# Fused attention and gated feed-forward on one core: another written-out order of 5,000 planned steps, other engines for some of them, and another replay behind the fill matmuls

## The chip, the core and the metric

The kernel is one program on one core of a Trainium2 chip. The metric is the device time of one execution in microseconds (us); lower is better. Five engines run their own instruction streams and wait for each other through semaphores: TensorE (PE in the rows; its weight loads are PEld), VectorE (DVE), ScalarE (ACT), GpSimd (POOL) and SyncE (SP), which here issues nearly all transfers.

## The reference

```
scores = q @ k.T / sqrt(64)                       # 8 batches x 8 heads, 576 x 576, head size 64
scores = where(scores >= max(scores) - tau, scores, -1e9)
attn   = exp(scores - max(scores));  attn /= sum(attn) + 1e-9
x = (attn @ v)  -> 4608 tokens x 512
h = x @ w_in                                      # 512 x 2048
g = h if h >= 1, 0 if h <= -1, else (h + 1)**2 / 4
out = g @ w_out                                   # 2048 x 512
```

q, k, v and the output are float32; w_in and w_out come as 64-bit floats.

## The kernel before, in words

Every operand of a matmul is split into a high and a low half-precision part, and each product is the sum of three matmuls (high x high, high x low, low x high). Only the four head pairs of batch 0 take their scores from plain float32 ("exact") products. Scales (powers of two, from sums of squares or from Gram matrices) are worked out for each operand before it is split.

**Attention.** The 8 heads of a batch are 4 pairs p; a pair fills 128 partitions. Scores come in *tiles* of 128 rows x 576, 288 in all (j = 0 to 287), two to a *visit* (144 visits). A tile passes smax (DVE: scale and minimum, L1127), sthr (DVE or ACT: threshold), sexp (ACT, L1137), smask (DVE: mask and sum, L1151), a normalisation, shi (ACT, high part, L1177), slo (low part, L1180) and a transposing DMA into eT (L1213). The letter of the tile in the table TILE says where normalisation and low part run: P (the default) normalises on POOL (snorm, L1169) after a reciprocal on DVE, and subtracts on POOL; N normalises on ACT after two small operations on DVE and subtracts on POOL; V takes the high part with the scale on ACT and the low part in one DVE instruction (lo_v, L1210). Then PE multiplies with V (L1299, "av"), and ACT and DVE write the result as two parts into an x buffer.

**V.** Four raw blocks of a batch (128 x 576, float32) are loaded, a scale is worked out (letter of the batch in SSQV: A = four squares on ACT with their sums, L685; G = Gram matrices on PE, L553, and a maximum on DVE, L691), and each block is split. Batch 0 is turned by PE instead (turn_v, L760, into the two score banks s0 and s1, evicted by ACT L765 and DVE L769).

**q and k** of batches 1 to 7 are scaled likewise (SSQ, one letter for each pair) and split: P on POOL (scale L645, low part L658), D with the low part on DVE (L656).

**Weights.** w_in and w_out come in 16 units of 512 KB each. ACT, POOL and DVE rebuild float32 from the bits (L853, L860, L862, L868, L870), PE takes Gram matrices (L881), one scale is worked out for each quarter of w_in and one for w_out (L786 to L794), and CONV says how each unit is split: A (scale and high part on ACT, L922 and L928; low part on POOL, L933), G (the same with scale and high part on POOL, L924 and L930), P and Q (high part on POOL, the difference by PE, L942 and L943, evicted by ACT, L949, or DVE), D (high part on POOL, L936, low part on DVE, L939) and M (scaled by PE, L952; ACT L955 and DVE L958 read it out).

**Feed-forward.** Tokens go in groups of 256. FFN1 (PE, ph<-x,WI) feeds relu and square (ACT L1376, L1379), the gate (DVE L1383) and its two parts (ACT L1388, DVE L1393); FFN2 (PE, acc<-WO) accumulates, ACT evicts (L1438) and SP stores. Before relu of batch b the factors fcs of the batch are needed (f_scale, five small operations, L1026 to L1030; letter in FSCALE: G on POOL, V on DVE).

**What sets the order.** Each step is an op of a planner (class Plan) with an engine, a cost, what it follows and which buffers it takes. The table ORDER lists all ops. The planner replays them in that order with its costs, and the program is written out sorted by the start times that this replay gives, so every engine executes its ops in that order. Where the replay shows TensorE idle for more than 0.4 us in the first 120 us, *fill matmuls* of ones x ones (keep_warm, L1454) are put in, 75% of the gap's length, into a bank of PSUM that is free there.

Of the kernel before, what the change touches and what calls it, by code (L numbers as in the profile page):

```python
# [24 lines left out]
XJ, XS = 1.2, 1.0  # L25

CONV = {"i": "AGAGGAGGPAGAADDP", "o": "PDDAADMGAAQGAGAD"}

# [1482 lines left out]
```

## Time and profile before

| | |
|---|---|
| three runs | 1097.62, 1098.51, 1099.12 us (median 1098.51) |
| profiled execution, first to last instruction | 1097.3 us (it has no other time of its own) |
| mean granted TensorE clock | 0.993 |
| PE busy | 1073.0 us, 98% |
| DVE, ACT, POOL busy | 906.1, 871.2, 759.4 us |
| fill matmuls | 314, of which 265 into the ph banks take 20.2 us |
| DMA | 155.88 MB moved, mean 142 GB/s |

The page says how long each engine worked, but the stages differ: in the first 40 us the transfers move nearly 400 GB/s, later less than half of that; and the three engines DVE, ACT and POOL, which have slack over the whole span, have little in the first 143 us. So the windows are read first, then the order of events in the first 143 us.

### The profile page before, as it was taken

The page shows a single profiled execution, that of the slowest core. Times are in us where ns is not written, and L with a number is a line of the kernel's source. Part 1 is how long each engine was busy: PE and PEld are TensorE (multiplying, and loading weights), DVE is VectorE, ACT ScalarE, POOL GpSimd, SP SyncE. Part 2 cuts the span into 40 slices and gives each one's busy share as a digit, 9 for nine tenths or more (in the row PEclk, how much of TensorE's full clock was granted, in tenths as well). Part 3 has the DMA queues.
Part 4 walks back from the last instruction along what each step waited for, and adds up shares of the span by engine and source line. Part 5 has one row for each costly group of instructions (what it writes and reads, how often), then busy time and mean ns, then how long its engine had stood idle before and what let it go on. Part 6 is the DMA issues. An engine that isn't in the chain of part 4 may idle for free.

```text
span 1097.3 us, 36713 instructions
## 1 busy us (share of the span) xinstructions
PE 1073.0 (98%) x14591; PEld 790.6 (72%) x14591; DVE 906.1 (83%) x2651; ACT 871.2 (79%) x1682; POOL 759.4 (69%) x880
## 2 busy tenths in 40 slices
PE   8799999999999999999999999999999999999998
PEld 7477668777777777776777677777786677767774
DVE  5899999999888888988898998888887899877223
ACT  5999989897888897887798888778788986776333
POOL 5999998786678785897668776576567885565000
PEclk9799999999999999999999999999999999999999
DMA  9997899775977887787778788569856676557000
GB/s 352 332 256 143 139 188 141 152 140 115 191 140 141 152 152 127 135 150 137 139 142 146 150 128 147 113 127 164 151 102 120 131 128 127 105 95 132 18 15 20
DMA packets 420668, 155.88 MB, mean 142 GB/s; under 512 B 399504, under 2 KB 399504, under 8 KB 420496
## 3 DMA queue, kind: packets, MB, share of 16 engines
q1 hardware_dynamic: 420416, 153.41, 71.7%
q8 instruction: 114, 1.87, 0.7%
q14 instruction: 58, 0.48, 0.2%
q10 hardware_dynamic: 80, 0.13, 0.0%
HBM read 45.09 MB, written 9.44 MB: 50 GB/s over the span
## 4 chain that ended last, share of the span: by engine, by line
PE 80%; DVE 10%; DMA 5%; POOL 2%; issue 2%; ACT 1%; SPq 0%; DVEq 0%; POOLq 0%; ACTq 0%
PE acc L466 30%; PE ph L466 30%; PE s L1073 9%; PE ph L1299 9%; DMA eT<-hl 2%; DVE s L1127 2%; DVE e L1151 2%; POOL hl L1180 1%; PE ph L1454 1%; DMA qq<-in_q_dram 1%; DMA kk<-in_k_dram 1%; DMA raw<-in_v_dram 1%; DVE ph L1383 1%; POOL e L1169 0%; DVE WO L939 0%
## 5 line engine op out<-in xcount | busy, mean ns | idle before, releaser
L466 PEld LDWEIGHTS <-WI 128*64 128x64 f16 (+1 forms) x7446 | 407.3, 108 | 55.1 <-issue 18.3
L1180 POOL TENSOR_TENSOR hl<-e,hl 128x576 f16<-128x576 f32 x267 | 347.3, 1309 | 107.7 <-ACT hl L1177 101.8
L466 PE MATMUL ph<-x,WI 128*64 128x256 f16 (+1 forms) x6912 | 400.6, 264 | 2.3 <-DVE x L1311 0.9
L1169 POOL TENSOR_SCALAR e<-e,sm 128x576 f32<-128x576 f32 x259 | 203.5, 790 | 106.6 <-DVE sm L1161 75.3
L1151 DVE SCALAR_TENSOR_TENSOR e<-s,sm,e 128x578 f32<-128x578 f32 x286 | 229.9, 812 | 21.6 <-ACT e L1137 17.0
L1137 ACT ACTIVATE e<-s,sm 128x576 f32<-128x576 f32 x288 | 208.5, 739 | 40.4 <-DVE s L1127 36.4
L1127 DVE TENSOR_SCALAR_CACHE_REDUCE s<-s,pc 128x576 f32<-128x576 f32 x252 | 203.5, 820 | 36.6 <-PE s L1073 35.3
L1177 ACT ACTIVATE hl<-e 128x576 f16<-128x576 f32 x267 | 178.2, 680 | 44.1 <-POOL e L1169 41.1
L466 PE MATMUL acc<-WO,ga 128*64 128x512 f16 (+1 forms) x1590 | 203.4, 380 | 0.0
L1073 PE MATMUL s<-kk,qq 64*128 64x288 f16 (+3 forms) x1840 | 152.1, 300 | 9.9 <-DMA qq<-in_q_dram 5.2
L466 PEld LDWEIGHTS <-ga 128*64 128x64 f16 (+1 forms) x1590 | 91.2, 109 | 82.3 <-issue 9.9
L1383 DVE SCALAR_TENSOR_TENSOR ph<-ph,fcs,asq 128x512 f32<-128x512 f32 (+1 forms) x160 | 111.7, 700 | 46.1 <-ACT asq L1379 44.9
L1376 ACT ACTIVATE asq<-ph,fcs 128x512 f32<-128x512 f32 (+1 forms) x160 | 116.1, 736 | 37.7 <-PE ph L466 36.9
L1299 PE MATMUL ph<-eT,vst 128*64 128x320 f16 (+2 forms) x1928 | 122.7, 279 | 2.9 <-DMA eT<-hl 2.0
L1299 PEld LDWEIGHTS <-vst 128*64 128x64 f16 x1928 | 100.2, 110 | 22.9 <-issue 7.9
L1073 PEld LDWEIGHTS <-qq 64*128 64x128 f16 (+1 forms) x1680 | 66.2, 96 | 48.3 <-issue 35.6
L1388 ACT ACTIVATE ga<-ph,fcs 128x256 f16<-128x256 f32 (+1 forms) x160 | 70.2, 450 | 29.2 <-DVE ph L1383 22.4
L1379 ACT ACTIVATE asq<-asq 128x512 f32<-128x512 f32 x144 | 90.3, 629 | 3.2
L1393 DVE SCALAR_TENSOR_TENSOR ga<-ph,fcs,ga 128x256 f16<-128x256 f32 (+1 forms) x160 | 70.5, 449 | 23.7 <-ACT WI L1388 8.3
L466 PE MATMUL acc<-WO,gb 128*64 128x512 f16 (+1 forms) x546 | 71.0, 379 | 0.0
L466 PE MATMUL acc<-WO 128*64 128x512 f16 (+1 forms) x546 | 69.4, 380 | 0.0
L466 PE MATMUL acc<-WO,WI 128*64 128x512 f16 (+1 forms) x534 | 68.2, 380 | 0.0
(189 smaller groups left out, 1162.5 us busy)
## 6 DMA issues: line engine op xcount, KB each, us to landing
raw<-in_v_dram SPq DMA_DIRECT2D x32, 288.0 KB, 3.5
WO<-in_moe_w_in_dram SPq DMA_DIRECT2D x16, 512.0 KB, 8.6
out_dram<-ob SPq DMA_DIRECT2D x32, 256.0 KB, 2.8
raw<-in_q_dram SPq DMA_DIRECT2D x28, 288.0 KB, 3.4
raw<-in_k_dram SPq DMA_DIRECT2D x28, 288.0 KB, 3.5
x<-in_moe_w_out_dram SPq DMA_DIRECT2D x10, 512.0 KB, 7.0
eT<-hl SPq DMA_TRANSPOSE x288, 3.5
WO<-in_moe_w_out_dram SPq DMA_DIRECT2D x4, 512.0 KB, 4.3
```

What stands on the lines that cost most here:

```text
L466: T.matmul(out[x], lhsT[:, x], rhs, **flags)
L1073: T.matmul(ap(sb, s_ps)[r, f, :SH], q, k, start=ql == kl == 0, stop=exact or ql == 1)
L1127: V.tensor_scalar(sv(), sv(), c, None, ALU.mult, ALU.min, accum_out=t[:, 0:1])
L1137: A.activation(ev(), sv(), AF.Exp, bias=ap(m, sm)[:, 0:1], scale=-1.0)
L1151: V.scalar_tensor_tensor(ev(SH + 1), sv(SH + 1), t[:, 2:3], ev(SH + 1), ALU.is_le, ALU.mult, accum_out=t[:, 3:4])
L1169: G.tensor_scalar(ev(), ev(), ap(m, sm)[:, 5:6], ESC, ALU.mult, ALU.mult)
L1177: A.activation(part2(0), ev(), AF.Copy)
L1180: G.tensor_tensor(part2(w), ev(), part2(0), ALU.subtract)
L1299: T.matmul(o[hd * D : (hd + 1) * D, :n], vt[:, k, hd * D : (hd + 1) * D], t[:, kb, (hd ^ p % 2) * n : ((hd ^ p % 2) + 1) * n], start=m == ...
L1376: A.activation(tv()[:, :, c], hv()[:, :, c], AF.Relu, bias=fcs[:, b, 2, q : q + 1], scale=fcs[:, b, 3, q : q + 1])
L1379: A.activation(ap(tb, asq), ap(tb, asq), AF.Square)
L1383: V.scalar_tensor_tensor(hv()[:, :, c], hv()[:, :, c], fcs[:, b, 0, q : q + 1], tv()[:, :, c], ALU.max, ALU.min)
```

## The change

All of ORDER is replaced, and so are the letters of the tables; the planner gets other costs and three more rules.

- **Letters.** CONV: units of kind A go from 12 to 7, G from 9 to 14, P from 3 to 1, Q from 1 to 0, D from 6 to 7, M from 1 to 3 (both weights together). TILE: N from 8 to 64 tiles, V from 19 to 27, P from 259 to 195 (among the 36 tiles of batch 0, which come first: N from 8 to 10, V from 3 to 2). The exact scores of batch 0 (visits 0 to 17) have 5 visits in two halves (S) instead of 9; of the others none instead of 2. QHOW now has a letter each for q and k: 25 of 64 are D, before it was 8 of 32 pairs, in batch 1 four of eight instead of two of eight. V gets its own table VHOW: G as before, A with the high part on ACT, P with scale and low part on POOL. SSQV: batch 0 takes its V scale from ACT instead of PE. SSQ: pairs 8 and 21 take theirs from Gram matrices on PE instead of ACT. FSCALE: batch 0 on DVE. SIGN and THR change too.
- **Replay.** The hop from one engine to the next depends on both; an op marked port (the low parts on DVE that read two SBUF operands: lo_v, the D parts of q, k and weights, V's) and any op of POOL exclude each other in time; after a long gap of TensorE that no free bank allows to be filled, its ops cost 85% more for 5 us.
- **Fill.** The first gap is filled to half of the former share; a bank that nobody takes later counts as free to the end. There are 403 fill matmuls instead of 314.

```
-XJ, XS = 1.2, 1.0
-CONV = {"i": "AGAGGAGGPAGAADDP", "o": "PDDAADMGAAQGAGAD"}
-PAIR = "SJSJSJSSJSSSSJJJJJSJJJJJJJJJJJJSJJJJJJJJJJJJJJJJJJJJJJJJJJJJJJJJJJJJJJJJJJJJJJJJJJJJJJJJJJJJJJJJJJJJJJJJJJJJJJJJJJJJJJJJJJJJJJJJJJJJJJJJJJJJJJJJ"
-QHOW = "DDPDPPDPPPDDPPPPPPPPPPPPPDDPPPPP"
+XJ, XS = 1.2, 1.17
+CONV = {"i": "GAGGGDGGPGGAADDA", "o": "GADMDGMGGAMGDAGD"}
+PAIR = "JJSSJJSJJSSJJJJJJJJJJJJJJJJJJJJJJJJJJJJJJJJJJJJJJJJJJJJJJJJJJJJJJJJJJJJJJJJJJJJJJJJJJJJJJJJJJJJJJJJJJJJJJJJJJJJJJJJJJJJJJJJJJJJJJJJJJJJJJJJJJJJJ"
+VHOW = "GGGGGPGGGPGGGGPGAAPAGGGAGGGG"
+QHOW = "DDDDPPDDPDPPDDDPPDPPPDPPDPDDPPPDPPPPPDPPPDDPPPDPPDPPDDPDPPPPPPPD"
...
 ORDER = [
-    0, 605, 606, 607, 608, 609, 12, 16, 13, 17, 1, 14, 18, 15, 19, 20, 21, 590, 592, 22, 23, 595, 580, 582, 591, 585, 587, 2, 593, 600, 611, 616, 596,
+    15, 19, 12, 16, 13, 17, 14, 574, 18, 0, 1, 20, 21, 847, 22, 584, 589, 585, 586, 576, 575, 577, 591, 23, 24, 26, 25, 579, 581, 38, 39, 41, 40, 42,
...
-SSQ = "AAAAAAAAAAAAAAAAAAAAAAAAAAAAAAAA"
-SSQV = "GAAAAAAA"
+SSQ = "AAAAAAAAGAAAAAAAAAAAAGAAAAAAAAAA"
+SSQV = "AAAAAAAA"
...
-FSCALE = "GGGGGGGG"
+FSCALE = "VGGGGGGG"
...
-    HOP = {"PE": 0.21, "DVE": 0.16, "ACT": 0.17, "POOL": 0.1, "SP": 0.08}
-    FREE, QUEUE, TURN, PAUSE = 0.18, 6.5, 0.097, (3.4, 2.2)
+    HOP = {
+        "PE": {"PE": 0.0, "DVE": 0.21, "ACT": 0.21, "POOL": 0.21, "SP": 0.21},
+        "DVE": {"PE": 0.15, "DVE": 0.14, "ACT": 0.17, "POOL": 0.24, "SP": 0.13},
+        "ACT": {"PE": 0.15, "DVE": 0.14, "ACT": 0.14, "POOL": 0.18, "SP": 0.14},
+        "POOL": {"PE": 0.08, "DVE": 0.08, "ACT": 0.06, "POOL": 0.12, "SP": 0.05},
+        "SP": {"PE": 0.12, "DVE": 0.08, "ACT": 0.05, "POOL": 0.08, "SP": 0.0},
+    }
+    FREE, QUEUE, TURN, PAUSE = 0.18, 6.5, 0.097, (3.4, 0.8)
...
-    def op(self, eng, cost, fn, after=(), take=(), uses=(), work=None, behind=None, mode=0):
+    def op(self, eng, cost, fn, after=(), take=(), uses=(), work=None, behind=None, mode=0, port=False):
 
         o = Op(eng, cost, fn, work, mode)
+        o.port = port
         o.n = len(self.ops)
...
+        busy, alone, slow = (0.0, 0.0), (0.0, 0.0), 0.0
         for o in self.ops:
             o.t = 0.0
         for o in (self.ops[n] for n in ORDER):
                 free[b.pool].remove(x)
                 b.slot, b.end = x[1], 0.0
                 t = max(t, x[0])
+            if o.port and t + o.cost > busy[0]:
+                t = max(t, busy[1])
+            elif o.eng == "POOL" and t + o.cost > alone[0]:
+                t = max(t, alone[1])
             o.t = t
             for b in o.take:
                 b.since = t
-            end = idle[o.eng] = t + o.cost
+            end = t + o.cost
+            if o.eng == "PE" and t < 120:
+                if t - idle["PE"] >= 2.2 and not any(x[0] <= idle["PE"] + 0.4 for p in ("ph", "acc", "s") for x in free[p]):
+                    slow = t + 5.0
+                if t < slow:
+                    end += 0.85 * o.cost
+            idle[o.eng] = end
+            if o.port:
+                alone = t, end
+            elif o.eng == "POOL":
+                busy = t, end
             if o.eng == "PE":
                 turn, mode = self.turned(mode, o.mode)
                 end = idle[o.eng] = end + self.TURN * turn
                     free[b.pool].append((b.end + self.FREE, b.slot))
                     self.held.append((b.pool, b.slot, b.since, b.end + self.FREE))
             for x in o.next:
-                x.t = max(x.t, end + (self.HOP[o.eng] if x.eng != o.eng else 0.0))
+                x.t = max(x.t, end + self.HOP[o.eng][x.eng])
...
-            def hi(rb=rb, tb=tb):
-                G.tensor_scalar(ap(tb, vb)[:, : 2 * S].rearrange("p (a s) -> p a s", a=2),
-                                ap(rb, raw)[:, None, :].to_broadcast([P, 2, S]), s[:, 2:3], 1.0, ALU.mult, ALU.mult)
-
-            def lo(rb=rb, tb=tb):
+            def norm(rb=rb):
+                G.tensor_scalar(ap(rb, raw), ap(rb, raw), s[:, 2:3], 1.0, ALU.mult, ALU.mult)
+
+            def hi(how, rb=rb, tb=tb):
+                t = ap(tb, vb)[:, : 2 * S].rearrange("p (a s) -> p a s", a=2)
+                r = ap(rb, raw)[:, None, :].to_broadcast([P, 2, S])
+                if how == "G":
+                    G.tensor_scalar(t, r, s[:, 2:3], 1.0, ALU.mult, ALU.mult)
+                elif how == "A":
+                    A.activation(t, r, AF.Copy, scale=s[:, 2:3])
+                else:
+                    A.activation(t, r, AF.Copy)
+
+            def lo(how, rb=rb, tb=tb):
                 t = ap(tb, vb)
-                V.scalar_tensor_tensor(t[:, 2 * S : 3 * S], ap(rb, raw), s[:, 2:3], t[:, :S], ALU.mult, ALU.subtract)
+                if how == "P":
+                    G.tensor_tensor(t[:, 2 * S : 3 * S], ap(rb, raw), t[:, :S], ALU.subtract)
+                else:
+                    V.scalar_tensor_tensor(t[:, 2 * S : 3 * S], ap(rb, raw), s[:, 2:3], t[:, :S], ALU.mult, ALU.subtract)
 
             def send(tb=tb, ob=ob):
                 Y.dma_start_transpose(ap(ob, vst), ap(tb, vb))
 
-            o1 = plan.op("POOL", 1.197, hi, [so], take=[tb], uses=[rb])
-            o2 = plan.op("DVE", 1.2 if b == 1 else 1.1, lo, [o1], uses=[rb, tb])
-            o3 = plan.op("SP", 1.65, send, [o2], take=[ob], uses=[tb], work=VSEND)
+            done = []
+            for how in plan.ways(("v", 4 * b + p - 4), VHOW[4 * b + p - 4], "GAP"):
+                o = plan.op("POOL", 0.712, norm, [so], uses=[rb]) if how == "P" else so
+                o = plan.op(*(("POOL", 1.197) if how == "G" else ("ACT", 1.14 if how == "A" else 1.05)), partial(hi, how), [o], take=[tb], uses=[rb])
+                done.append(plan.op(*(("POOL", 1.25) if how == "P" else ("DVE", 0.7)), partial(lo, how), [o], uses=[rb, tb], port=how != "P"))
+            o3 = plan.op("SP", 1.7, send, [plan.join(done)], take=[ob], uses=[tb], work=VSEND)
...
-            gap = WARM[2] * (o.t - free)
+            gap = WARM[2] * (o.t - free) * (0.5 if free < 3 else 1)
             if o.t - free > WARM[0] and o.t < WARM[1]:
                 until = {}
                 for p, x, bank in banks:
-                    until[p, x] = min([t0 for q, y, t0, t1 in plan.held if (q, y) == (p, x) and t1 > free] + [o.t])
+                    until[p, x] = min([t0 for q, y, t0, t1 in plan.held if (q, y) == (p, x) and t1 > free] + [1e9])
```

The first ACTIVATE rows of ACT, as the program lists them. Before (ph, WO and x are stages of weight units, vst and s the turned V of batch 0):

```order
L862 ACT_TABLE_LOAD
L862 ACTIVATE ph0_63<-WO_68 128x512
L503 ACTIVATE junk_128<-ones_129 128x1
L853 ACTIVATE ph2_65<-WO_68 128x512
L853 ACTIVATE WO_68<-WO_68 128x512
L862 ACTIVATE ph0_63<-WO_68 128x512
L853 ACTIVATE ph1_64<-WO_68 128x512
L765 ACTIVATE vst0_85<-s0_61 128x512
L765 ACTIVATE vst0_85<-s0_61 64x128
L853 ACTIVATE ph2_65<-WO_68 128x512
```

And now, at the same place (line numbers are those of the changed kernel, 21 to 37 higher):

```order
L707 ACT_TABLE_LOAD
L707 ACTIVATE junk_128,vssq_143<-raw0_69 128x576
L707 ACTIVATE junk_128,vssq_143<-raw1_70 128x576
L707 ACTIVATE junk_128,vssq_143<-raw2_71 128x576
L707 ACTIVATE junk_128,vssq_143<-raw3_72 128x576
L525 ACTIVATE junk_128<-ones_129 128x1
L890 ACTIVATE WO_68<-WO_68 128x512
L899 ACTIVATE ph1_64<-WO_68 128x512
L890 ACTIVATE ph2_65<-WO_68 128x512
L899 ACTIVATE ph0_63<-WO_68 128x512
L802 ACTIVATE vst0_85<-s0_61 128x512
L802 ACTIVATE vst0_85<-s0_61 64x128
```

The four squares of V now stand ahead of all weight units on ACT; on PE the four Gram matrices of V are gone.

The queue of SP from the first load of q or k to the load of the third pair's q (qq_82; kk and qq are the four exact pairs, raw the blocks of V, WO and x stages of weight units). Before, behind 8 weight units and the 4 blocks of V:

```order
L571 DMA kk_76<-in_k_dram 128x576
L571 DMA qq_80<-in_q_dram 128x576
L839 DMA WO<-in_moe_w_in_dram 128x1024 x3
L571 DMA qq_81<-in_q_dram 128x576
L571 DMA kk_77<-in_k_dram 128x576
L839 DMA WO<-in_moe_w_in_dram 128x1024
L839 DMA x_107<-in_moe_w_out_dram 128x1024
L839 DMA x_105<-in_moe_w_out_dram 128x1024
L839 DMA WO<-in_moe_w_in_dram 128x1024 x3
L571 DMA kk_78<-in_k_dram 128x576
L571 DMA qq_82<-in_q_dram 128x576
```

And now, behind the 4 blocks of V, which come first of all, and 7 weight units:

```order
L593 DMA qq_80<-in_q_dram 128x576
L535 DMA tcs<-in_tau_dram 128x1
L593 DMA qq_81<-in_q_dram 128x576
L593 DMA kk_76<-in_k_dram 128x576
L876 DMA WO<-in_moe_w_in_dram 128x1024 x2
L876 DMA x_105<-in_moe_w_out_dram 128x1024
L876 DMA WO<-in_moe_w_in_dram 128x1024
L593 DMA kk_77<-in_k_dram 128x576
L593 DMA kk_78<-in_k_dram 128x576
L876 DMA WO<-in_moe_w_in_dram 128x1024
L593 DMA qq_82<-in_q_dram 128x576
```

Up to and with qq_82 the queue held 8 + 3 + 1 + 2 + 3 = 17 weight units of 512 KB and 4 + 6 = 10 blocks of 288 KB; now it holds 7 + 2 + 1 + 1 + 1 = 12 units and the same 10 blocks.

## Rows read from the trace of the kernel before

**Rows 1.** Windows of the span: busy us (instructions), granted clock, DMA share, GB/s.

```profile
0.00:20.00 20.00, 17.20 (x209) 15.46 (x210) 7.93 (x22) 9.22 (x18) 8.95 (x47) 1.00 0.92 336
20.00:40.00 20.00, 14.02 (x113) 10.13 (x110) 17.86 (x56) 18.57 (x35) 17.45 (x22) 0.84 1.11 395
40.00:60.00 20.00, 16.66 (x173) 12.26 (x172) 18.16 (x64) 18.76 (x36) 19.31 (x22) 0.81 1.06 292
60.00:100.00 40.00, 37.18 (x551) 29.93 (x549) 36.82 (x111) 38.33 (x82) 38.27 (x53) 1.00 0.89 187
100.00:143.00 43.00, 40.45 (x419) 27.10 (x418) 40.78 (x113) 39.09 (x75) 41.26 (x40) 1.00 0.91 158
143.00:1098.00 955.00, 947.46 (x13141) 695.67 (x13138) 784.60 (x2291) 747.24 (x1442) 634.13 (x700) 1.00 0.69 127
```

**Rows 2.** Who PE waited for from 143 us to the end.

```profile
PE ph L1299 <- DMA eT<-hl: 1.6, 3, 0.8
PE s L1073 <- DVE e L1151: 0.5, 2, 0.3
```

**Rows 3.** Timeline of SP from 1 to 3 us: start, us, what.

```profile
1.20 1.83 SPq L680 DMA_DIRECT2D raw<-in_v_dram  x4
```

**Rows 4.** DMA issues from 1.1 to 3.1 us: KB each, median us to landing.

```profile
raw<-in_v_dram SPq DMA_DIRECT2D x4, 288.0 KB, 5.6
```

**Rows 5.** Timeline of PE, first 60 us.

```profile
10.91 0.65 PE L553 MATMUL ph<-raw 128*128 128x128 bf16 x5
...
35.78 3.27 PE L1073 MATMUL s<-kk,qq 64*128 64x288 f32 x8 [5.21 <-DMA qq<-in_q_dram]
```

**Rows 6.** Timeline of DVE at the scale of V.

```profile
11.60 0.29 DVE L691 TENSOR_REDUCE vssq<-ph 128x1 f32<-128x128 f32 x1 [3.07 <-PE ph L553]
```

**Rows 7.** Timeline of POOL: first split of a weight, first f_scale.

```profile
21.69 0.69 POOL L924 TENSOR_SCALAR WI<-WI,wsc_i 128x512 f32<-128x512 f32 x1 [2.68 <-DVE wsc_i L794]
...
63.60 0.26 POOL L1026 TENSOR_SCALAR scs<-scs,wsc_i 128x1 f32<-128x1 f32 x1
...
64.78 0.22 POOL L1030 TENSOR_TENSOR fcs<-wsc_i,fk 128x16 f32<-128x16 f32 x1
```

**Rows 8.** Groups by line: count, busy us, mean ns of one, idle before.

```profile
L1180 POOL TENSOR_TENSOR hl<-e,hl 128x576 f16<-128x576 f32 x267 | 347.3, 1309 | 107.7 <-ACT hl L1177 101.8 <-issue 4.1 <-POOL e L1169 0.7
...
L1454 PE MATMUL ph<-ones 128*128 128x128 bf16 x265 | 20.2, 237 | 2.9 <-POOL ones L487 2.8
...
L685 ACT ACTIVATE junk<-raw 128x576 f16<-128x576 f32 x28 | 19.2, 685 | 1.4 <-DMA raw<-in_v_dram 1.4
...
L685 ACT ACTIVATION_READ_ACCUMULATOR junk<-raw 128x1 f32 x28 | 5.6, 202 | 0.0
...
L922 ACT ACTIVATE WI<-WI,wsc_i 128x512 f32<-128x512 f32 x6 | 4.3, 712 | 1.0 <-DVE wsc_i L794 1.0
...
L924 POOL TENSOR_SCALAR WI<-WI,wsc_i 128x512 f32<-128x512 f32 x6 | 4.2, 697 | 2.8 <-DVE wsc_i L794 2.7
...
L928 ACT ACTIVATE WI<-WI 128x512 f16<-128x512 f32 x6 | 3.7, 622 | 0.2
...
L939 DVE SCALAR_TENSOR_TENSOR WO<-WO,wsc_o 128x512 f16<-128x512 f32 x4 | 5.9, 1463 | 0.1
...
L939 DVE SCALAR_TENSOR_TENSOR WI<-WI,wsc_i 128x512 f16<-128x512 f32 x2 | 1.6, 804 | 0.0
...
L958 DVE TENSOR_TENSOR WO<-ph,WO 128x512 f16<-128x512 f32 x1 | 0.7, 684 | 0.0
```

**Rows 9.** V's low part on DVE, all instructions: ns min/median/max, first and last start.

```profile
L733 DVE SCALAR_TENSOR_TENSOR vb<-raw,scs,vb x28: 798/854/1940, 111.7 to 939.2; 128x576 f16<-128x576 f32 x28
```

**Rows 10.** Timeline of PE from 60 to 100 us.

```profile
65.38 2.10 PE L1073 MATMUL s<-kk,qq 64*128 64x288 f32 x8
...
80.07 1.54 PE L881 MATMUL acc<-WO 128*128 128x128 bf16 x24
...
82.84 1.24 PE L1073 MATMUL s<-kk,qq 64*128 64x288 f32 x8
```

More of the change, by code (lines that the diff above doesn't have):

```diff
@@ L660, in add_qk @@
             o2, o3 = [], []
-            for how in plan.ways(("qk", at), QHOW[at], "PD"):
-                o1 = plan.op("POOL", 0.724, norm, [sc1], uses=[rb, cb]) if how == "P" else sc1
-                o2.append(plan.op("ACT", 0.582 if how == "P" else 0.67, partial(hi, how), [o1], take=[nb], uses=[rb, cb]))
-                o3.append(plan.op(*(("POOL", 1.245) if how == "P" else ("DVE", 0.8)), partial(lo, how), [o2[-1]], uses=[rb, nb, cb]))
+            for how in plan.ways(("qk", 2 * at + n), QHOW[2 * at + n], "PD"):
+                o1 = plan.op("POOL", 0.712, norm, [sc1], uses=[rb, cb]) if how == "P" else sc1
+                o2.append(plan.op("ACT", 0.573 if how == "P" else 0.666, partial(hi, how), [o1], take=[nb], uses=[rb, cb]))
+                o3.append(plan.op(*(("POOL", 1.25) if how == "P" else ("DVE", 0.7)), partial(lo, how), [o2[-1]], uses=[rb, nb, cb], port=how != "P"))
             o2, o3 = plan.join(o2), plan.join(o3)
@@ L707, in add_v @@
                 for p in range(NPAIR):
-                    o = plan.op("PE", 0.29, partial(gram, p), [loads[p], o], take=[] if p else [sb], uses=[bufs[p], sb])
+                    o = plan.op("PE", 0.487, partial(gram, p), [loads[p], o], take=[] if p else [sb], uses=[bufs[p], sb])
                 o = plan.op("DVE", 0.2, largest, [o], uses=[sb])
@@ L769, in lo @@
                     V.tensor_tensor(t[:r, nk + k0 : nk + k1], view()[:r, k0:k1], t[:r, k0:k1], ALU.subtract)
-                h = plan.op("ACT", (k1 - k0) * P / 1200 + 0.05, hi, [o], take=[] if k0 else [ob], uses=[tb, ob], behind=h)
+                h = plan.op("ACT", (k1 - k0) * P / 1200 + 0.062, hi, [o], take=[] if k0 else [ob], uses=[tb, ob], behind=h)
                 done.append(plan.op("DVE", (k1 - k0) * P / 960 + 0.065, lo, [h], uses=[tb, ob]))
@@ L908, in add_w @@
                 gbuf = plan.buf("acc")
-            stats.append(plan.op("PE", 0.243, gram, [o4], take=[gbuf] if not u else [], uses=[gbuf], behind=stats[-1] if stats else None))
+            stats.append(plan.op("PE", 0.232, gram, [o4], take=[gbuf] if not u else [], uses=[gbuf], behind=stats[-1] if stats else None))
         wscale[w] = []
@@ L974, in add_w @@
                     if how == "D":
-                        done.append(plan.op("DVE", 1.1, rest2, [o]))
+                        done.append(plan.op("DVE", 0.66, rest2, [o], port=True))
                         seen.append(done[-1])
@@ L1213, in send @@
             Y.dma_start_transpose(whole(i)[:, : 2 * w // P, col : col + P], ap(x, hl)[:, : 2 * w])
-        o = plan.op("DVE", 0.908, smax, [o, c2], take=[m], uses=[s, cb] if cb else [s])
-        o2 = plan.join([plan.op(*(("DVE", 0.135) if how == "V" else ("ACT", 0.19)), partial(sthr, how), [o], uses=[m])
+        o = plan.op("DVE", 0.745, smax, [o, c2], take=[m], uses=[s, cb] if cb else [s])
+        o2 = plan.join([plan.op(*(("DVE", 0.13) if how == "V" else ("ACT", 0.18)), partial(sthr, how), [o], uses=[m])
                         for how in (plan.ways(("thr", j), THR[j], "VA") if j < 64 else "V")])
-        o = plan.op("ACT", 0.64, sexp, [o], take=[e], uses=[s, m])
+        o = plan.op("ACT", 0.624, sexp, [o], take=[e], uses=[s, m])
         take = [eTb[i]] if new else []
```

68 lines of the change are left out of this document (34 added, 34 removed), and 399 rows, old and new, of the table ORDER.

## The prediction

> **What bounds the kernel now.** I read the windows first [rows 1]. From 143 us on PE is busy 947.5 of 955 us, and DVE, ACT and POOL have 170 us of slack or more each. Who PE waited for there [rows 2] adds up to 2.1 us in 955; of the 7.5 us that PE is not busy, the rest is the drain behind the last matmul. So from 143 us on the time is PE's work and nothing else. What can change it is how much of PE's work is done by 143 us, and how much work PE has.
>
> Ahead of that the same windows show another stage. In the first 20 us the transfers run at 336 GB/s, then at 395, while DVE, ACT and POOL have about half of the time or less to do: they wait for data. From 20 to 143 us the three are all full: of 123 us DVE is busy 113.6 (17.86 + 18.16 + 36.82 + 40.78), ACT 114.8 and POOL 116.3, so they are idle 9.4, 8.2 and 6.7 us. PE is busy 14.0 of 20 and 16.7 of 20 us at first, with fill matmuls in it, at a granted clock of 0.84 and 0.81 of full speed, that is, part of these stretches at 1.2 instead of 2.4 GHz; then it lacks 2.8 us in 60 to 100 and 2.6 in 100 to 143. The reader is to see that PE's gaps before 60 us are a symptom: three other engines prepare its operands and cannot go faster.
>
> **The change, part by part.** All terms are in us against the profiled execution, 1097.3 from first to last instruction; the median of the runs is 1.2 above it, and I add the sum to the median, 1098.5.
>
> *The start: -2.5.* The blocks of V are now first in the queue, not behind a 512 KB unit: 0.52 MB at 336 GB/s [rows 1], 1.6 us earlier. They were issued from 1.20 on over 1.83 us [rows 3] with 5.6 to the landing [rows 4], so the last was in by about 8.6; but its Gram matrix ran on PE at 10.91 for 0.65 [rows 5], behind fill matmuls, and the maximum at 11.60 for 0.29 [rows 6]. Now ACT squares each block, 0.685 + 0.202 [rows 8]; three of the four lie under the landing of the next, and the last takes 0.89, as long as the last Gram matrix and its maximum did (0.94). So V's scale comes 1.6 to 1.6 + 2.3 = 3.9 earlier, the 2.3 being 10.91 - 8.6. Behind it stand V's turn, then the conversions of the first quarter of w_in on ACT and DVE, then that quarter's scale, for which POOL waits 2.68 until 21.69 [rows 7]: the first point where all three engines are full. The other end is 0, if the units themselves are late there. The squares cost ACT 3.5, covered by its 10.8 idle us in that window; if a block of V landed late, the weight units behind it on ACT would be late with it. I take 2.5, near the middle.
>
> *The third pair's loads: -0.8.* Up to qq_82 the queue held 17 units and 10 blocks, 11.9 MB; now 12 and 10, 9.2 MB. At 395 GB/s [rows 1] 2.6 MB are 6.6 us, more than the 5.21 that PE waited at 35.78 for this q [rows 5]. The wait goes, and with it a cause of the half clock. But the engines that are full lose little by it: between 20 and 60 us ACT, the fullest, is idle only 2.7. So the range is -2.7 to 0, and I take a third of it. What is late instead is w_in's last unit, which the queue now issues behind the first transpose.
>
> *Work moved between the three full engines: +1.0.* Counted up to 143 us, with durations of rows 8. ACT: five units fewer in way A, 5 x (0.712 + 0.622) = -6.7; two P evictions fewer and two M readings more cancel; tiles +0.7: -6.0. POOL: five more in way G, about 5 x (0.697 + 0.62) = +6.6; the first f_scale, 1.4 from 63.60 to 64.78 + 0.22 [rows 7], goes to DVE; two high parts fewer, -1.4; one half of q or k fewer by then, -(0.70 + 1.31); tiles +0.6: +2.4. DVE: f_scale +1.4; M two more and Q one fewer, +0.68; one D more, +0.80 (1.46 by the row for w_out); a low part of q or k, +0.85, and one of a tile less, -0.85 [rows 9]; small operations of the N tiles at most +0.6; V's maximum -0.29: +3.2. Together nothing (-0.4), but DVE's idle time would fall from 9.4 to 6.2 and POOL's from 6.7 to 4.3. The cover is this idle time; without it DVE's +3.2 would be paid in full. Range 0 to +3.2, I take a third.
>
> *The low parts.* V's low part took 854 ns in the median and 1940 at most [rows 9]; four on w_out units took 1463 in the mean, two on w_in 804 [rows 8]: beside POOL they can be late, mostly they are not. The Trainium skill (SBUF — State Buffer, Who interferes with whom) says that a VectorE instruction with two SBUF inputs and a GpSimd instruction that reads SBUF exclude each other, and the second waits for all of the first. By that rule the two added low parts could each wait out a subtraction on POOL of 1.31, and the sum would be 2.6 higher, 1097.6. The median speaks against paying it each time.
>
> *PE's work ahead of 143 us: -1.3.* Exact visits in halves took 2.10, whole ones 1.24 [rows 10]; three of the four that change (visits 7, 11 and 12) come after FFN1 has begun: 3 x 0.86 = -2.6 if PE were the bound there, 0 if not. Half.
>
> *PE's waits from 60 to 143 us: -1.5.* They are 2.8 + 2.6 = 5.4 [rows 1]. A new order can close them or open as many as in the second window: -5.4 to +2.6.
>
> *The fill matmuls: 0.* 89 more at 20.2 / 265 = 0.076 are 6.8. They lie in gaps, 75% of a gap at most; where a gap is not there, what is queued behind them on PE is a score product and with it DVE's smax. Before 60 us the full engines hide that.
>
> *PE's work behind 143 us: +1.6.* Two Gram matrices each for pairs 8 and 21, 20 matmuls of 128 columns, where nothing hides them: 24 such took 1.54 [rows 10], five in the start 0.65 [rows 5], so 1.3 to 2.6. The 56 more N tiles, the ways of V and the other D letters move work between engines with 170 us of slack: 0.
>
> Sum: -2.5 - 0.8 + 1.0 - 1.3 - 1.5 + 1.6 = -3.5, so 1095.0.
>
> **The rivals.** *No change.* What the start gains is spent in the full engines (they need their 123 us and their idle time is made of short hand-overs, not of slack), and PE comes to its backlog at the same time. Left are -1.3 and +1.6: 1098.8. For it: all three above 92% busy. Against: POOL's 2.68 at the start is one long wait on a chain that does get shorter.
>
> *Slower: DVE becomes the bound.* Place: 40 to 143 us. Price: +3.2 unabsorbed, and the two added low parts at 1.46 instead of 0.80 beside POOL, 2 x 0.66 = +1.3, with +1.6 behind, less the start's 2.5: +3.6, 1102.1. It decides from the point where DVE's idle time in 20 to 143 us falls under about 4 and PE waits for score banks that DVE has not freed.
>
> *More than forecast.* PE's 5.4 between 60 and 143 close: -2.5 - 0.8 - 5.4 - 1.3 + 1.6 = -8.4, 1090.1. Against: the three engines would have to reach 97%.
>
> **How the numbers follow.** Forecast 0.42 (its own range 1092 to 1097), no change 0.27, slower 0.17, more 0.14. A measurement of this kernel tells 0.2%, 2.2 us, from no change. Faster: nearly all of the forecast (0.38) and the last rival, 0.52; slower: its rival and a tail of the second, 0.21; the same: 0.27. The range reaches into the rivals at both ends, 1090 to 1101.
>
> **What would show it.** POOL's first weight split before 20.5 instead of at 21.69, else the start term is wrong. The third pair's product before 31 and no PE wait for qq; the granted clock of 20 to 60 us nearer 1.00. PE continuously busy 3 to 4 us earlier against the same work: I would compare the start of the first FFN1 of the second token group. DVE's idle time in 20 to 143 near 6; under 4 speaks for the slower rival. Behind 143 us PE's waits about 2; if they are over 5, the new letters of the later tiles matter and the forecast is wrong for a reason that it does not contain.

## The result: 6.6 us slower, and the profile after

The changed kernel takes 1105.0 us (median; 1103.5 to 1106.1), the kernel before 1098.5 beside it: a ratio of 1.0061 with a 95% interval of 1.0048 to 1.0074. The forecast was 1095.0. The same program measured again (changed_again, below) gave 1.0059 (1.0046 to 1.0071). The profiled execution has a span of 1103.9 us, 6.6 more than before, at the same mean clock (0.993).

Its windows, which answer to [rows 1], with the same columns:

```profile
core 0: us, PE busy (x) PEld busy (x) DVE busy (x) ACT busy (x) POOL busy (x), PEclk, DMA share, GB/s
0.00:20.00 20.00, 15.39 (x166) 13.67 (x167) 7.04 (x22) 12.19 (x26) 8.43 (x47) 1.00 0.90 332
20.00:40.00 20.00, 16.96 (x219) 13.72 (x216) 18.43 (x56) 16.16 (x31) 18.88 (x24) 1.00 1.01 341
40.00:60.00 20.00, 17.32 (x176) 12.53 (x173) 16.54 (x55) 17.27 (x32) 17.36 (x21) 0.83 0.98 266
60.00:100.00 40.00, 34.20 (x496) 27.67 (x494) 36.64 (x109) 37.26 (x79) 37.46 (x44) 0.91 1.06 223
100.00:143.00 43.00, 40.92 (x463) 27.69 (x464) 42.13 (x121) 39.89 (x78) 42.46 (x43) 1.00 0.80 139
143.00:1098.00 955.00, 949.98 (x13104) 697.45 (x13103) 795.65 (x2373) 791.89 (x1499) 550.90 (x618) 1.00 0.71 128
```

From 20 to 40 us the clock is full now, but from 40 to 100 us all three of DVE, ACT and POOL do less than before. The clock is still partly at half from 40 to 60 us (0.83, before 0.81), and now also from 60 to 100 us (0.91). POOL's work behind 143 us has gone to ACT and DVE, as the letters say. Who PE waits for behind 143 us, which answers to [rows 2]:

```profile
engine line waited for: us in total, times, longest us
PE s L1110 <- DVE e L1188: 2.0, 6, 0.7
PE ph L488 <- ACT junk L623: 1.0, 1, 1.0
PE ph L1336 <- DVE pc L654: 0.9, 1, 0.9
```

The first is a score product that waits for a bank which DVE's mask (L1188) has not freed; it was 0.5. All of PE's waits there add up to 4.6 us, before to 2.1. Two places of the timeline, POOL's first split and the third pair's product, answer to [rows 7] and [rows 5], and two more are the first FFN1 of the first and of the second token group:

```profile
19.19 0.69 POOL L961 TENSOR_SCALAR WI<-WI,wsc_i 128x512 f32<-128x512 f32 x1 [4.39 <-DVE wsc_i L831]
```

```profile
32.77 0.72 PE L1110 MATMUL s<-kk,qq 64*128 64x288 f32 x2 [0.69 <-issue]
...
74.07 0.33 PE L488 MATMUL ph<-x,WI 128*128 128x128 f16 x3
...
163.76 0.39 PE L488 MATMUL ph<-x,WI 128*64 128x256 f16 x4
```

In the kernel before those two stand at:

```profile
69.75 0.33 PE L466 MATMUL ph<-x,WI 128*128 128x128 f16 x3 [0.21 <-DVE WO L870]
...
161.60 0.39 PE L466 MATMUL ph<-x,WI 128*64 128x256 f16 x4
```

So what the start gains is lost by 74 us (+4.3) and half regained by the second group (+2.2); from there to the end of the last matmul it takes 935.6 us instead of 931.2, another 4.5. The profile of changed_again, the same program, has 72.60 and 162.56 at the two places and 935.3 behind them: the places ahead of the second group are uncertain by 1 to 1.5 us from one execution to the next, and the larger and steadier part of the loss lies behind it.

### The profile page after: what moved, and what is told of

Same layout as the page of the kernel before. It is cut to its first block, busy times and chain, and to the rows that moved or that the text cites. A ratio compares the mean times of both kernels' runs of the same rounds, so it can differ in the third digit from the quotient of the medians.

```text
span 1103.9 us, 36826 instructions
## 1 busy us (share of the span) xinstructions
PE 1076.2 (97%) x14613; PEld 793.2 (72%) x14613; DVE 916.4 (83%) x2731; ACT 915.4 (83%) x1742; POOL 675.5 (61%) x792
## 4 chain that ended last, share of the span: by engine, by line
PE 76%; DVE 9%; ACT 4%; POOL 4%; issue 3%; DMA 3%; SPq 0%; DVEq 0%; POOLq 0%; ACTq 0%
PE acc L488 30%; PE ph L488 28%; PE s L1110 9%; PE ph L1336 8%; DVE s L1164 2%; DVE e L1188 2%; POOL hl L1217 1%; ACT e L1174 1%; DMA raw<-in_v_dram 1%; POOL e L1206 1%; ACT hl L1214 1%; DMA WO<-in_moe_w_in_dram 1%; DVE ph L1420 1%; DMA x<-in_moe_w_out_dram 1%; DVE hl L1247 0%
## 5 line engine op out<-in xcount | busy, mean ns | idle before, releaser
L1217 POOL TENSOR_TENSOR hl<-e,hl 128x576 f16<-128x576 f32 x259 | 334.6, 1300 | 170.9 <-ACT hl L1214 150.6
L488 PE MATMUL ph<-x,WI 128*64 128x256 f16 (+2 forms) x6840 | 400.3, 264 | 0.6 <-DVE pc L654 0.5
L1188 DVE SCALAR_TENSOR_TENSOR e<-s,sm,e 128x578 f32<-128x578 f32 x286 | 231.2, 816 | 28.6 <-ACT e L1174 19.0
L1206 POOL TENSOR_SCALAR e<-e,sm 128x576 f32<-128x576 f32 x195 | 147.3, 759 | 109.9 <-DVE sm L1198 59.9
L1214 ACT ACTIVATE hl<-e 128x576 f16<-128x576 f32 x259 | 174.0, 680 | 16.5 <-POOL e L1206 14.7
L1110 PE MATMUL s<-kk,qq 64*128 64x288 f16 (+3 forms) x1840 | 149.2, 299 | 7.5 <-DVE e L1188 5.7
L488 PE MATMUL acc<-WO,WI 128*64 128x512 f16 (+1 forms) x558 | 70.7, 380 | 0.0
L488 PE MATMUL acc<-WO 128*64 128x512 f16 (+1 forms) x510 | 66.4, 380 | 0.0
```

What stands on the lines that cost most here:

```text
L488: T.matmul(out[x], lhsT[:, x], rhs, **flags)
L1110: T.matmul(ap(sb, s_ps)[r, f, :SH], q, k, start=ql == kl == 0, stop=exact or ql == 1)
L1188: V.scalar_tensor_tensor(ev(SH + 1), sv(SH + 1), t[:, 2:3], ev(SH + 1), ALU.is_le, ALU.mult, accum_out=t[:, 3:4])
L1206: G.tensor_scalar(ev(), ev(), ap(m, sm)[:, 5:6], ESC, ALU.mult, ALU.mult)
L1214: A.activation(part2(0), ev(), AF.Copy)
L1217: G.tensor_tensor(part2(w), ev(), part2(0), ALU.subtract)
```

## The experiments

All ratios are to the kernel before, run beside each kernel on the same chip. The changed kernel's own is 1.006.

**Single suspects of the first 74 us, and the letters of later tiles.** Four places looked guilty in the trace: f_scale on DVE at 63.8 us with PE waiting 1.43 and 1.91 behind it, a load that held SP's queue for 4.9 us, the Gram matrices, and the N tiles.

```
-SSQ = "AAAAAAAAGAAAAAAAAAAAAGAAAAAAAAAA"      squares_only
+SSQ = "AAAAAAAAAAAAAAAAAAAAAAAAAAAAAAAA"
-FSCALE = "VGGGGGGG"                            f_scale_pool
+FSCALE = "GGGGGGGG"
 ORDER: load of w_in unit 13 and its steps      load_behind
-  640, 633, 642, 641, ... 623, 643, ... 11, 636,
+  633, ... 623, ... 11, 636, 640, 641, 642, 643,
-TILE = {... 44: "N", 55: "N", 60: "N", ...}    late_tiles_p
+TILE = {... (54 tiles from 44 on back to P)}
```

> The changed kernel with the squares of pairs 8 and 21 back on ACT, so that PE has no Gram matrix of q or k any more (20 matmuls of 128 columns fewer). If the Gram matrices cost PE what they take there, 1.96 us by the starts of the matmuls, the time falls by 1.5 to 2.5 us, 1105.0 to about 1103.0. If they stand in waits that are there anyway, or if the squares (2 x 2 of about 0.67 us) make ACT late for something that PE waits for, the time stays within 0.7 us of 1105.0.

> The changed kernel with the first f_scale on GpSimd, as before the change. If its 1.4 us on DVE at 63.8, ahead of the masks of tiles 10 to 12, make PE wait (1.43 at 63.87 and 1.91 at 66.98) and with it the half clock from 65.4 on, the first FFN1 starts 2 to 4 us before 74.07 and the time falls by 1.5 to 3. The rival: the three engines are late by that time anyway, since the third quarter of w_in came late; then the wait moves to POOL, whose splits are 1.4 us later, the first FFN1 starts within 1 us of 74.07, and the time changes by under 1 us.

> The changed kernel with one load, w_in's unit 13, issued behind the loads of units 9, 10 and 12 and of the last k, and its conversions behind theirs. In the changed kernel it holds the queue for 4.9 us (18.9 to 23.96), since its place in memory is free only when DVE has converted unit 5. If this stall is what makes w_in late (last quarter's scale done at 52.0 instead of 50.9) and brings the half clock at 48.4, then DMA in 20 to 40 us goes from 341 back to near 390 GB/s, the first FFN1 starts 2 to 4 us before 74.07, and the time falls by 1.5 to 4. The rival: the engines have no room for the data anyway; then the transfers are earlier, but the first FFN1 starts within 1 us of 74.07 and the time changes by under 1 us.

> The changed kernel with 54 of the N tiles from tile 44 on back in way P (the normalisation on GpSimd instead of ACT), those that were not N before the change. If ACT's added 0.67 us for each makes PE wait for score banks and evictions behind 163 us (2.6 us more in the score products than before), the time falls by 1.5 to 3 us. The rival: the order itself, not the letter, puts the waits there; then the time stays within 0.7 us of 1105.0. Nothing ahead of 100 us should change, the first FFN1 stays at 74.1.

Measured: 1.0075 (1.0062 to 1.0088), 1.0069 (1.0055 to 1.0082), 1.0070 (1.0057 to 1.0082) and 1.0323 (1.0309 to 1.0337). None of the first three is the cause: the time did not move. That the first FFN1 came 0.5 to 1.7 us earlier in them says little, as it came 1.5 earlier in changed_again too, where nothing was edited. (The replay, run with the edited table, also put 66 more fill matmuls into f_scale_pool.) The fourth was wrong in sign by far, +28 us: this order does not bear the other letters. The kernel's own replay would have said so without a run: it plans the end of late_tiles_p at 1109.3 us and that of the changed kernel at 1082.7. Who PE waits for behind 143 us in late_tiles_p and in squares_only:

```profile
PE s L1110 <- DVE e L1188: 10.9, 18, 1.5
PE ph L1336 <- DMA eT<-hl: 4.7, 2, 4.0
PE ph L488 <- DVE x L1348: 3.4, 5, 1.2
```

```profile
PE ph L488 <- ACT junk L623: 4.3, 3, 2.3
PE s L1110 <- DVE e L1188: 1.6, 4, 0.7
```

What one engine is given there, PE waits for, although DVE, ACT and POOL each have 159 us or more without work behind 143 us. In late_tiles_p all its waits there add up to 23.9 us instead of 4.6, and PE's own work behind the second group takes 942.3 us instead of 932.3, some 10 of them at half clock. In squares_only the Gram matrices' time comes back as waiting for the squares on ACT (4.3).

**The half clock.** In the changed kernel's first profile the clock fell to half among PE's gaps at 46.6 to 49.0 us, and again among those at 62.4 to 67.0, and visit 4's product at 51.29 took 2.29 us, where whole ones took 1.24 [rows 10].

```
-FSCALE = "VGGGGGGG"                                             filled_pool
+FSCALE = "GGGGGGGG"
+FILL = {649: 1.2, 654: 0.4, 103: 1.3, 47: 0.6, 3829: 0.3}     # us of fill ahead of a PE step
+FILL = {922: 4.6, 694: 0.3, 645: 0.35, 945: 1.1, 62: 0.55, 1198: 0.8, 3850: 0.7}   before_filled
```

> The changed kernel with the first f_scale on GpSimd and with 61 more fill matmuls, put by hand where PE waited at 46.6 to 49.0, at 98 and at 118 us. The theory of the half clock: after these waits PE ran at 1.2 GHz, visit 4's product took 1.09 us too long, the reading of unit 8 0.99, visit 6's product 1.11, the third AV 0.91, and the order passes each on to every engine; with the gaps filled the first FFN1 starts at 70.5 or before instead of 74.07, and the second token group at 161.5 or before instead of 163.76; the time falls by 2 to 3 us, ratio to before about 1.004. The rival: what is gained there is lost again in other waits before the second group starts, as when f_scale alone was moved (first FFN1 1.3 us earlier, second group 0.4 later); then the ratio stays at 1.006 to 1.007.

> The kernel before with 91 more fill matmuls in the 5.21 us in which PE waited for the third pair's q at 35.78, and in 0.6 us at 58.7. If the half clock of 33.8 to 40.6 us delays what ends the stage, the first FFN1 starts 1 us or more before 69.75 and the time falls by 1 to 2 us. If the order of before has slack there, so that such delays are caught up by 60 us, as its engines do (0.2 us ahead of plan at 42, 1.6 behind at 56, 1.0 at 64), the time stays within 0.7 us of before.

filled_pool: 1.0055 (1.0043 to 1.0067). Its clock is full from 20 us on:

```profile
20.00:40.00 20.00, 16.96 (x211) 13.64 (x210) 18.36 (x57) 15.60 (x31) 18.51 (x24) 1.00 0.97 352
40.00:60.00 20.00, 18.22 (x220) 13.82 (x219) 18.78 (x58) 19.02 (x35) 18.79 (x23) 1.00 1.12 243
60.00:100.00 40.00, 36.61 (x578) 30.75 (x578) 34.49 (x102) 36.81 (x77) 37.83 (x48) 1.00 1.02 235
```

and the second group still starts 142.6 us behind the first score product (165.24 - 22.65), as in the changed kernel (163.76 - 21.38 = 142.4); before it is 139.1. The theory of the half clock falls. The profile of changed_again says the same: its clock was full from 40 to 60 us, and its ratio is 1.0059.

```profile
40.00:60.00 20.00, 16.80 (x211) 12.27 (x208) 18.77 (x59) 19.19 (x35) 18.87 (x23) 1.00 1.01 265
```

before_filled (1.0086, 1.0073 to 1.0099) says nothing on it: the added fill matmuls had to wait 6.19 us for their bank, and the product behind them came at 43.22 instead of 35.78.

**Replay or order.** The order of before in the changed replay, the changed order in the replay of before, and the former with before's fill matmuls put back; per engine the sequence of steps is unchanged in each.

```
 before_new_replay: changed kernel with ORDER and all letters of before (VHOW = "G" * 28, each QHOW letter twice)
 after_old_replay:  HOP, costs, order() and gaps() of before under the changed ORDER and letters
 before_old_fills:  before_new_replay, 298 of before's 314 fill matmuls at their places by hand
```

> The order and all letters of before in the changed kernel's replay: every engine has the same operations in the same sequence as before, and only what the replay decides differs, the buffers' slots and the fill matmuls (84 fewer). If the replay itself costs time, through fewer fills at the start or other slots, this is 1 us or more slower than before. If the new order and letters alone are to blame, it is within 0.7 us of before.

> The new order and letters in the replay of before, with its costs, slots and fill matmuls (497 instead of 403); every engine has the same operations in the same sequence as in the changed kernel. With the order of before in the new replay (ratio 1.0034) this completes a table of two by two. If replay and order add up, this is at 1.0027 or so to before. If the new replay suits only its own order, or the fills decide, it is at 1.006 or above.

> The order of before in the new replay as in the run with ratio 1.0034, but with the fill matmuls of before put at their places by hand (298 of 314 found a free bank), so that what differs from before is the slots alone. If it was the missing fills (clock 0.73 to 0.78 of full speed from 40 to 80 us) that cost 3.7 us there, this is within 0.7 us of before. If the slots or the place of the instructions in the program cost it, it stays at 1.002 or above.

Measured: 1.0034 (1.0022 to 1.0046), 1.0065 (1.0053 to 1.0078), 1.0028 (1.0018 to 1.0039). The changed order is equally slow in either replay: order and letters alone are enough for the whole loss, whatever replay runs them. The two do not add up: the order of before loses 3 to 4 us by the new replay alone, the changed order nothing. The missing fills do not explain that loss, as 1.0028 with them is within the intervals of 1.0034 without. What does, the slots or something else, stays open.

**The low parts beside GpSimd.** What did the three full engines lose? The changed trace at 116 us, DVE and then POOL:

```profile
115.48 0.80 DVE L1188 SCALAR_TENSOR_TENSOR e<-s,sm,e 128x578 f32<-128x578 f32 x1
116.21 0.08 DVE L1188 DVE_READ_ACCUMULATOR e<-s,sm,e 128x1 f32 x1
116.21 1.60 DVE L976 SCALAR_TENSOR_TENSOR WO<-WO,wsc_o 128x512 f16<-128x512 f32 x1
117.73 0.47 DVE L1430 SCALAR_TENSOR_TENSOR ga<-ph,fcs,ga 128x256 f16<-128x256 f32 x1
...
116.11 1.15 POOL L970 TENSOR_TENSOR WO<-WO 128x512 f16<-128x512 f32 x1
117.24 1.18 POOL L1206 TENSOR_SCALAR e<-e,sm 128x576 f32<-128x576 f32 x1
118.39 1.27 POOL L1217 TENSOR_TENSOR hl<-e,hl 128x576 f16<-128x576 f32 x1
```

The low part of a w_out unit (L976, two inputs in SBUF) is issued at 116.21 and takes 1.60, where the shortest took 0.745: POOL's subtraction runs until 117.26, and the low part ends 0.55 behind it (117.81). POOL's next instruction starts at 117.24, takes 1.18 instead of 0.75 and ends 0.61 behind the low part (118.42). Each looks held until the other is nearly through. The mask (L1188), which reads PSUM and one SBUF input, is not held. Behind 163 us the same reaches PE, here the rows of DVE, POOL and PE:

```profile
363.91 1.28 POOL L1217 TENSOR_TENSOR hl<-e,hl 128x576 f16<-128x576 f32 x1 [0.53 <-ACT hl L1214]
...
364.04 1.76 DVE L1247 SCALAR_TENSOR_TENSOR hl<-e,sm,hl 128x576 f16<-128x576 f32 x1
365.73 0.20 DVE L1171 TENSOR_SCALAR sm<-sm,tcs 128x1 f32<-128x1 f32 x1
366.03 0.82 DVE L1188 SCALAR_TENSOR_TENSOR e<-s,sm,e 128x578 f32<-128x578 f32 x1
...
366.91 0.65 PE L1110 MATMUL s<-kk,qq 64*64 64x288 f16 x13 [0.65 <-DVE e L1188]
```

A low part that takes a microsecond too long makes the mask late, and with it the bank. The experiment takes the second SBUF input away in each kernel (lines of the four kinds of low part; the subtraction is left out):

```
-V.scalar_tensor_tensor(lo, src, s, hi, ALU.mult, ALU.subtract)
+V.tensor_scalar(lo, hi, 1.0, None, ALU.mult, ALU.min, accum_out=spare)
```

> The changed kernel in which each low part that VectorE makes reads one input from SBUF instead of two (its high part times 1, with a running minimum; the subtraction is left out). Nothing else moves. In the changed kernel the low parts took up to 1.85 us instead of 0.81, and GpSimd operations beside them up to 0.55 longer: 10.0 us of DVE and 12.4 of POOL in excess of the shortest ones from 60 us on. The theory: the order has no room for these, the first score product to the second token group takes 142.4 us of which about 10 are this; then the excess goes to nearly 0, that stretch falls to 133 to 136 us, and the kernel is 6 to 11 us faster than the changed one, 1094 to 1099. The rival: the excess lies in time that the engines would wait in anyway; then the stretch stays at 140 or more and the time falls by under 3.

> The kernel before with the same edit of the low parts (the subtraction is left out). It has 15.9 us of excess on DVE and 24.4 on POOL from 60 us on. The theory: this order was searched with low parts of 0.8 to 1.2 us, so that it has room for the excess; it gains clearly less than the changed kernel does by the same edit, under 4 us (first score product to second token group now 139.1). The rival: the exclusion costs both orders alike; then both gain the same within 1.5 us.

(The changed kernel's 10.0 and 12.4 are from 100 us on; from 60 on they are 10.5 and 13.2. The excess is summed over operations over 0.15 us longer than the shortest tenth of their kind.) Measured: 0.9993 (0.9984 to 1.0001) and 0.9979 (0.9969 to 0.9988). Low parts and POOL's subtractions in the changed kernel (min/median/max in ns), and in its one-input form:

```profile
L976 DVE SCALAR_TENSOR_TENSOR WO<-WO,wsc_o x4: 745/1292/1602, 103.0 to 139.1; 128x512 f16<-128x512 f32 x4
...
L1247 DVE SCALAR_TENSOR_TENSOR hl<-e,sm,hl x27: 799/818/1765, 104.4 to 1015.4; 128x576 f16<-128x576 f32 x27
...
L1217 POOL TENSOR_TENSOR hl<-e,hl x259: 1269/1279/1798, 35.4 to 1013.5; 128x576 f16<-128x576 f32 x130
```

```profile
L977 DVE TENSOR_SCALAR_CACHE_REDUCE WO<-WO x4: 668/680/682, 100.1 to 134.4; 128x512 f16<-128x512 f16 x4
...
L1248 DVE TENSOR_SCALAR_CACHE_REDUCE hl<-hl x27: 732/747/755, 100.9 to 1006.8; 128x576 f16<-128x576 f16 x27
...
L1218 POOL TENSOR_TENSOR hl<-e,hl x259: 1272/1279/1299, 35.0 to 1005.0; 128x576 f16<-128x576 f32 x130
```

The excess is gone on both engines. PE's waits for banks behind 143 us fall from 2.0 to:

```profile
PE s L1111 <- DVE e L1189: 0.3, 2, 0.2
```

The changed kernel gains 7.5 us by it (1.0061 to 0.9993, 0.0068 of 1098), the one before 2.3. So 5.2 of the 6.6 us go with the exclusion (the three intervals leave some 2 us to either side). The pair squares_early and squares_early_one_input, below, shows the gain in the changed order once more: 1.0073 to 1.0002, 7.8 us. It is not that the changed kernel is held for longer: its excess, 10.5 and 13.2, is smaller than that of the kernel before, 15.9 and 24.4. Its order bears the excess worse. Whether another relief of DVE and POOL by as much would help the changed order as much was not tried. The first score product to the second group falls from 142.4 to 137.1 (158.03 - 20.96) in the changed kernel, from 139.1 to 136.3 in the other. The edit also shortens an unhindered low part by about 0.06 us, in both kernels alike.

**What is left, and another way to make low parts.** Squares three to five places earlier on ACT, the same with one input, 16 of 20 Gram matmuls left out, the Gram matrices in the order of before; and the low parts of four w_out units from PSUM (way M).

```
-SSQ = "AAAAAAAAAAAAAAAAAAAAAAAAAAAAAAAA"            before_grams
+SSQ = "AAAAAAAAGAAAAAAAAAAAAGAAAAAAAAAA"
 ORDER of squares_only: 119, 120, 362, 363 earlier    squares_early, squares_early_one_input
-for x in [0, full, *range(P, full, P)]:              fewer_grams (its start and stop flags follow)
+for x in [0]:
-CONV["o"] = "GADMDGMGGAMGDAGD"                       after_m_units (before_m_units likewise)
+CONV["o"] = "GAMMMGMGGAMGMAGM"
```

> The kernel before with the squares of pairs 8 and 21 as Gram matrices on PE, the one part of the change that adds work to PE behind 163 us. If PE pays for them in full, the time rises by 1.6 to 2.2 us (20 matmuls that took 1.96 in the changed kernel). If they stand in waits, or spare ACT something that PE waits for, it stays within 0.7 us of before.

> The changed kernel with the squares of pairs 8 and 21 on ACT as in the run before (1.0075), but three to five places earlier in ACT's order, since PE waited 1.95 and 2.58 us for them there. If the Gram matrices cost PE their own time in this order too (1.96 us by the starts of the matmuls), the time falls by 1.5 to 2.5 us against the changed kernel, ratio to before 1.004 to 1.005. The rival: something else sets the pace behind 163 us; then the ratio stays at 1.006 or above.

> The same and the low parts with one SBUF input (the subtraction is left out). If exclusion and Gram matrices together are the whole difference between the two kernels, this is as fast as the kernel before with one input, 0.9979, or faster (0.996 to 0.998), since the start is 1.2 us earlier. The rival: a part of the difference lies elsewhere; then it stays near 0.9993.

> The changed kernel with the Gram matrices of pairs 8 and 21 over 128 of 576 positions only (16 of 20 matmuls are left out, so that their norms are too small). No other engine has more or less to do. If PE's time behind 163 us counts in full, it is 1.6 us faster than the changed kernel in the same call, up to 2. If the matmuls stand in waits, it is within 0.5 us of it.

> The changed kernel as it is, for the direct comparison: 1.006 to before, as at first (1.0048 to 1.0074).

> The changed kernel with the four w_out units of way D in way M: PE scales them into PSUM, ACT makes the high part, VectorE the low part from PSUM and one SBUF input. Their low parts took 1233 ns in the mean and POOL was held beside them. If the exclusion is what these cost, the time falls by 1 to 3 us (1.0035 to 1.0055). The rival: the 4 x 0.95 us on PE and 4 x 0.5 on ACT ahead of 143 us take it back; the ratio stays at 1.006 or above.

> The kernel before with its four w_out units of way D in way M, and a few neighbours on PE, DVE and ACT in other places because of it. Its low parts there took 1463 ns in the mean. If this order has room for them, as its gain of 2.3 us by one input says, the time is within 1 us of before or up to 1.5 faster; if PE's and ACT's added work comes on top, it is 1 to 3 us slower.

before_grams: 1.0030 (1.0019 to 1.0040), +3.3 us, more than the matmuls take. Behind the second group PE is busy 931.2 us there instead of 928.9 and idle 3.0 instead of 2.2. squares_early: 1.0073 (1.0061 to 1.0086), no gain. Its table lists the steps nearly in the order of time, with each engine's sequence unchanged but for the squares, and its replay puts in 77 more fill matmuls. PE now waits more for masks and still for squares; whether ACT, loaded with the squares, is late with what the masks need, is not shown:

```profile
PE s L1110 <- DVE e L1188: 3.9, 10, 0.8
PE ph L488 <- ACT junk L623: 1.8, 2, 1.4
```

squares_early_one_input: 1.0002 (0.9992 to 1.0013), not the 0.997 expected. fewer_grams: 1.0072 (1.0058 to 1.0085) beside 1.0059 (1.0046 to 1.0071) of the changed kernel: no gain in the runs (the profiled spans, 1100.9 and 1102.4, are of single executions, that of fewer_grams its fastest). So the Gram matrices cost 3.3 us in the order of before, and in the changed order I could not show by a run that they cost anything.

The two one-input profiles tell where the last 1.4 us of the difference may lie. The changed kernel is 0.6 us ahead at the second group (158.03, the other 158.63) and needs 3.0 more from there to the last matmul's end (932.95, the other 929.98). Of these PE is busy 2.0 longer (930.6, 928.6) and idle 0.9 longer, and 20 Gram matmuls took 1.96. That fits them as the rest, but squares_early_one_input, without them, did not bear it out: it saves 1.4 behind the second group (931.53) and reaches it 1.9 later (159.89). So they stay open.

after_m_units and before_m_units: 1.0140 (1.0126 to 1.0154) and 1.0149 (1.0133 to 1.0164). They are 9 and 16 us slower than the kernels that they change; the second group starts at 170.95 and 173.31. That is far more than the 3.8 us on PE and 2.0 on ACT that were counted as added work; the kernels' own replays plan the second group that late (171.4 and 173.0), but which step makes it late no run shows. This edit does not buy the exclusion off. No kernel that computes the whole beat the one before.

## Why the prediction was wrong

**The step that failed is the low parts, taken as 0** (by the rule that was cited there, +2.6); the runs show some 5.2 us for them. Row and rule were in the text, and I let the median of 854 ns speak against the rule. A median says that most low parts run free; the sum is made by those that do not, and by the POOL instructions held behind them, which I did not count at all. And I priced only the two low parts that the change adds, not how the whole new order bears the ones that are there. The Trainium skill (SBUF — State Buffer, Who interferes with whom) says that such a pair excludes each other for the whole instruction; the trace agrees (1.60 and 1.18 at 116 us), and with one input no instruction is held.

Why the changed order suffers more is read from its text, not from a run. Its replay compares an instruction with the last one of the other engine in the table's sequence, not in time. Worked out with the kernel's own costs, the rule moves no step ahead of 290 us in the changed table: the first FFN1 of the second group is planned at 153.0, with the rule or without it, and of the low parts planned ahead of 143 us every one lies on top of an instruction of POOL. The table of squares_early, which has the same sequences per engine up to there but lists the steps nearly in the order of time, has no such overlap there and gives 164.5 in the same replay; the trace has 163.76. The table of before, made with low parts of 0.8 to 1.2 us, gives 159.3 in its own replay, and the trace has 161.60. So the changed table planned without the time that the exclusion takes, where before it stood in the costs. That fits the two gains of 7.5 and 2.3; it was not tried with a new search. The exclusion is not all that the plan lacks: with one input the changed kernel reaches the second group at 158.03, still 5.0 behind its plan. And the rule in the order of time is no exact measure: an estimate for the table of before, gone through in that way, comes out at about 167, too late by 5 or 6.

**The start, -2.5:** POOL's first split did come 2.5 earlier. But the first score product, which I did not follow, came only 1.1 earlier (21.38, before 22.47), and by the first FFN1 nothing of it was left. **The third pair, -0.8:** the wait for q went and the clock was full, as forecast, but the product came at 32.77, not before 31; by visit 4 0.7 was left (51.29, before 52.00). **Work between the full engines, +1.0:** from the first score product to the second group DVE was busy for 130.9 us (before 129.2), ACT 127.8 (130.1), POOL 132.9 (133.1), so that the amounts were right in sign for DVE and ACT, but smaller. Idle time did not take them up: it rose to 11.5, 14.6 and 9.5 from 9.9, 9.0 and 6.1. That it is made of hand-overs between engines, as the rival of no change said, fits; no run shows it. **PE's work ahead of 143 us, -1.3:** no run separates it. **PE's waits, -1.5:** of the 5.4 us not busy from 60 to 143, the windows now show 7.9 (5.80 + 2.08). **Work behind 143:** the Gram matrices, +1.6, measured +3.3 in the order of before; in the changed order their cost is not shown. That the letters "move work between engines with 170 us of slack: 0" was wrong as an argument: taking 54 of them back cost 28 us, 19 of them in PE's waits, which slack over 955 us did not prevent. **The fill matmuls, 0:** as forecast; the changed order is as slow with 403 as with 497.

The rival on the slower side named DVE as the bound and gave 1102.1; its sign was right, and it held a part of the cause, two low parts late beside POOL at +1.3. Its test was not right: DVE's idle time from 20 to 143 us is 9.3, not under 4, and still the kernel is slower. Of the other signs that were named, the second group's first FFN1 came 2.2 later, not 3 to 4 earlier, and PE's waits behind 143 us are 4.6, twice the 2 that were expected and just under the 5 that would have told against the letters.

## What to carry to other kernels

Where VectorE and GpSimd are both full, count the instructions of either that are longer than their shortest, and weigh the sum of the excess, not the median. An order searched against a model is only as good as the model where it is tight: compare its planned times with the trace at a few points (153.0 against 163.8 here) before believing its gain. Slack summed over a long stage is no cover for an in-order queue: 54 steps of 0.7 us given to another engine made PE wait for 19 us more and the kernel 28 us slower.

## What the runs showed of the hardware that was not expected

POOL pays more than DVE: from 60 us on its instructions were 13.2 us longer in the changed kernel (DVE's 10.5), 24.4 in the one before (15.9), and all of it went when DVE's low parts read one SBUF input. The half clock was not fixed by the program: with the same gaps of 1.5 and 0.5 us ahead of it PE ran at half clock from 48.4 us in the changed kernel's first profile, and at full clock (1.00 from 40 to 60 us) in changed_again, the same program. The first split of thirteen kernels with the changed start lay between 18.0 and 20.5 us, so that a single profile tells a start to no better than 1 us.
